# Two of a pair's score groups become one, in an attention and MoE kernel whose order is planned by slots

## The chip, the cores and the metric

The kernel runs on one core of a Trainium2 chip. The metric is the device time of one execution in microseconds; shorter is better.

## The reference

For 4 batches and 8 heads, with 576 tokens and 64 values a head, the kernel computes causal softmax attention and a read of a memory, mixes them by a gate of each head, and sends the result through two products with a gelu between them.

```python
scores = where(causal, -1e9, q @ k.T / sqrt(64))
a = exp(scores - scores.max(-1)); a /= a.sum(-1) + 1e-9
local = a @ v
q_p = where(q > 0, q, exp(q) - 1) + 1
mem_out = (q_p @ M_prev) / (q_p @ z_prev + 1e-6)
x = g * mem_out + (1 - g) * local        # g = sigmoid(beta), one for each head
h = x @ w_in                             # 2304 x 512 by 512 x 2048
out = (h * sigmoid(1.702 * h)) @ w_out   # 2048 to 512
```

All inputs and the output are float32; the two weights reach the kernel as 64-bit words, from which it decodes float32 itself.

## The kernel before

Attention is worked in 16 pairs of heads (4 batches, 4 pairs in each). The two heads of a pair lie on the two halves of the partitions, so that the scores of head 0 and of head 1 use the upper and the lower 64 rows of TensorE and can run beside each other. A pair's queries are cut in blocks of 128: block `i` (0 to 3) sees `128 * (i + 1)` keys, and the last 64 queries of both heads form a tail of 288 + 288 keys. For the first batch blocks 0 and 1 are done by a separate start, so its four pairs (0 to 3, called `rest` in the code) have only blocks 3 and 2 and the tail.

For each block there are scores into a bank of PSUM for each head (`s_both`, tile `ps`), a masked maximum on DVE (`max_unit`, line 560, tile `nm`), an exponential with its sum on ACT (`exp_unit`, line 566, tile `a`), the reciprocal of the sum on DVE (`inv_unit`, tile `sm`), and a scaling on POOL (`scale_unit`, line 569). Then the blocks are transposed on TensorE in units named 0 to 3, "b", "c" and "d" (`tr_unit`, line 139, tile `pt`), each unit in a bank, and copied to SBUF (`ev_unit`, tiles `e`, `eb`, `ec`, `ed`) by DVE ("V") or ACT ("A"). Last come the values (`pv_both`, tile `po`): those for queries 256 on with `js` 0 to 3, then those for queries 0 to 255 with `js` -1. `xboth` takes them from PSUM into a high part `xh` (ACT) and a low part `xl` (DVE).

The first MoE product (tile `pm`, called fill) runs between: eight chunks of 256 or 320 tokens, 16 blocks of w_in (tile `wi`) each, 12 matmuls a block, copied out as `hk` and stored. A chunk can start when the four pairs of its batch have their values. After attention the rest of the fill runs, then the second product (tile `acc`, line 1019).

Order is planned by slots. A pair `p` starts at slot `k0`; pairs 0 to 3 are 7 slots apart, later ones 8. `at(slot, priority, fn)` puts work in a slot. After the events of a slot, fill is handed out until the planner's estimate of TensorE's time for that slot is reached (`PACE`: 2.2 us before slot 60, 2.8 after). Each group of scores counts 0.3 us in that estimate beside its matmuls, and a transpose 0.109. The order in which each engine gets its instructions is then made by a scheduler that simulates the engines; a group has a raised priority, and its matmuls are chained in order. For the chunk of number 1, fill may not run more than four slots ahead.

`scores` (line 719) makes a group: it takes the banks (`s_rooms`), waits with its first matmul for the evictions of the banks before (`rooms(KEEP)`, all but the last one), and takes the values handed on by `hand_on` (line 728) for the pair before behind its own matmuls. Those values wait for all the copies `ev` that they read. `flush` makes a group of values that no scores have taken. The score and transpose banks are four (`ps_s`), and from slot 35 on a fifth (`ps_x`).

Of the kernel before, what the change touches and what calls it, by code (L numbers as in the profile page):

```python
# [34 lines left out]
def tile_attention_memory_moe(ctx, tc, kq, vq, mem, zz, beta, w_in, w_out, out):  # L35
# [46 lines left out]
    def bank(name):  # L82
        state["bank"] += 1
        own = state["slot"] > CONV[-1] + 8 and state["bank"] % 5 == 4
        t = (ps_x if own else ps_s).tile([128, 512], F32, name=name, tag="ps")
        banks.append(id(t))
        held[id(t)] = t
        return t
# [7 lines left out]
    def rooms(keep):  # L96
        return [users[k] for k in banks[:len(banks) - keep][-6:] if k in users]
# [5 lines left out]
    def group(fns, behind):  # L103
        state["group"] = []
        with tc.high_priority(offset=400):
            for fn in fns:
                fn()
        seq = state.pop("group")
        for name in behind:
            if name is not None:  # L110
                tc.add_manual_dep(seq[0].ins, name, SYNC, reason="group")
        for a, b in zip(seq, seq[1:]):
            tc.add_manual_dep(b.ins, a.ins.name, NOSYNC, reason="group")
        state["pe"] += 0.3

    def at(slot, prio, fn):
        assert slot > state["slot"], (slot, state["slot"])
        state["seq"] += 1
        events.setdefault(slot, []).append((prio, state["seq"], fn))
# [451 lines left out]
    def plan_attend(p):  # L571
        b, c = pairs[p]
        k0 = K0[p]
        P = prep[p]
        U = {}
        rest = b < MB
        qo = 256 if rest else 0

        def s_rooms(blocks):
            names = rooms(KEEP)  # L580
            ps = [bank("ps") for _ in range(2)]
            for h in range(2):
                for i in blocks:
                    o = 256 if i == 0 else 0
                    U["ps", h, i] = ps[h][:, o:o + 128 * (i + 1)]
                    U["in", h, i] = ps[h]
            return names

        def s_both(i):
            n, q0 = 128 * (i + 1), S + 128 * i - qo  # L590
            kq = raws[p]["kq"]
            for h in range(2):
                r = slice(64 * h, 64 * h + 64)
                mm(U["ps", h, i], kq[r, q0:q0 + 128], kq[r, :n], True, True)

        def max_unit(h, i):
            n = 128 * (i + 1)
            U["nm", h, i] = softmax_max([(U["ps", h, i][:, :n], n, mask[:, 512 - n:])])

        def exp_unit(h, i):  # L600
            n = 128 * (i + 1)
            if h == 0:
                state["sum"] = (state["sum"] + 1) % 8
                U["sm", i] = sums[state["sum"]]
            if i == 3:
                a = wkp.tile([128, 512], F32, name="a3", bufs=4)
            elif i:
                t = U["t", h, i] = wkp.tile([128, 384], F32, name="a2", bufs=5)
                a = t[:, :n]
            else:  # L610
                a = U["t", h, 1][:, 256:]
            U["a", h, i] = a
            x = softmax_exp(U["ps", h, i][:, :n], a, U["nm", h, i], U["sm", i][:, h, :1])
            used(U.get(("in", h, i), U["ps", h, i]), x)
            state["exp"] = state["late A"] = x.ins.name

        def inv_unit(i):
            sm = U["rs", i] = sml.tile([128, 2], F32, name="sm")
            nc.vector.tensor_reduce(out=sm, in_=U["sm", i], op=ALU.add, axis=AX.X)
            nc.vector.reciprocal(out=sm, in_=sm)  # L620

        def scale_unit(h, i):
            hh = 2 * c + h
            scale_rows(U["a", h, i], U["rs", i][:, h:h + 1], g1[:, hh:hh + 1])
# [42 lines left out]
        def ev_unit(u, eng):  # L667
            n, pt = 128 * len(blocks_of(u)), U["pt", u]
            e = U["e", u] = att.tile([128, n], F32, name=f"e{u}")
            x = copy(eng, e, pt[:, :n])  # L670
            used(pt, x)
            U["ev", u] = state["late " + eng] = x.ins.name
# [32 lines left out]
        def xboth(ch):  # L705
            n = 2 * b + ch
            if n not in xq:
                new_x(n)
            values["po"] = split_sum(n, c, U["po", ch][:, :chunks[n][2]]).ins.name
            if c == NP - 1:  # L710
                xplan[n] = state["slot"] + 1
# [7 lines left out]
        def scores(blocks):  # L719
            names = s_rooms(blocks)  # L720
            late = values.pop("next", None)
            fns = [lambda i=i: s_both(i) for i in blocks]
            if late is not None:
                fns += late[0]
                names = names + late[1]
            group(fns, names)

        def hand_on(js, pv, names):
            values["next"] = ([lambda j=j: pv(j) for j in js], names + [values.get("po")])
# [3 lines left out]
            if late is not None:  # L733
                group(*late)

        for i, idx in ((3, 1), (2, 5)) if rest else ((3, 1), (2, 4), (1, 5), (0, 5)):
            if i:
                at(k0 + idx, 20, lambda i=i: scores((1, 0) if i == 1 else (i,)))
            k = k0 + idx
            for h in range(2):  # L740
                at(k + 1, 10, lambda h=h, i=i: max_unit(h, i))
                at(k + 1, 25, lambda h=h, i=i: exp_unit(h, i))
            at(k + 1, 90, lambda i=i: inv_unit(i))
            for h in range(2):
                at(k + 2 + (h if i >= 2 else 0), 10, lambda h=h, i=i: scale_unit(h, i))
        units = [(0, 8, "V"), (1, 8, "A"), (2, 9, "V"), (3, 9, "A"), ("b", 10, "V"), ("c", 11, "A")]
        if not rest:
            units.append(("d", 12, "V"))
        for u, k, eng in units:
            at(k0 + k, 20, lambda u=u: tr_unit(u))  # L750
            at(k0 + k, 24, lambda u=u, eng=eng: ev_unit(u, eng))
        for js, us, k in ((range(4), (0, 1, 2, 3, "b", "c"), 12), ((-1,), ("c", "d"), 13))[:1 if rest else 2]:
            at(k0 + k, 12, lambda js=js, us=us: hand_on(js, pv_both, [U["ev", u] for u in us]))
            at(k0 + k, 30, flush)
            at(k0 + k, 32, lambda ch=int(js != (-1,)): xboth(ch))
# [84 lines left out]
    for p in range(NPAIRS):  # L840
        plan_prep(p)
        plan_attend(p)
# [113 lines left out]
    units = [(gr, s, p) for gr in range(NG) for s in range(7) for p in range(4)]  # L956
# [82 lines left out]
    k = 0  # L1039
    while fill["gen"] is not None or conv_q or events:  # L1040
# [4 lines left out]
        if k in soon:  # L1045
            t, p = soon[k]
# [120 lines left out]
```

## Time and profile before

| | us |
|---|---|
| median of 3 runs | 608.57 |
| lowest, highest | 608.16, 611.19 |
| the profiled execution | 608.29 |
| its span, first to last instruction | 606.4 |

| engine | busy us | share of the span |
|---|---|---|
| PE (TensorE matmul) | 579.6 | 96% |
| PEld (its weight loads) | 522.4 | 86% |
| DVE | 417.8 | 69% |
| ACT | 348.3 | 57% |
| POOL | 215.9 | 36% |

Times in rows are microseconds from the start of the span. Matmuls are pipelined, so the busy time of a row of them is longer than the step from its start to the start of the next row; the step is what a piece of work takes from the queue. The granted clock of TensorE is 1.00 of full speed in every stretch from 36 us on. Attention runs to about 366 us, the rest of the fill to about 425, the second product to the end.

### The profile page before, as it was taken

What the parts mean: (1) busy time and instruction counts of PE and PEld (TensorE: products, weight loads), DVE (VectorE), ACT (ScalarE), POOL (GpSimd) and SP (SyncE); (2) the same over time, 40 slices, a digit from 0 to 9 for tenths busy, and PEclk for the clock granted to TensorE, in tenths of its full rate; (3) what the DMA queues carried; (4) which work ended last, traced back from release to release, by engine and by line L of the source; (5) the groups of instructions that cost most, each with busy time, mean ns of one, the idle gap of its engine ahead of it and who ended that gap; (6) DMA issues with size and microseconds to landing.
All of it is one profiled execution on the core that took longest, in us unless ns stands there. A gap on an engine that the chain in (4) does not pass through costs nothing.

```text
span 606.4 us, 12121 instructions
## 1 busy us (share of the span) xinstructions
PE 579.6 (96%) x4416; PEld 522.4 (86%) x4416; DVE 417.8 (69%) x998; ACT 348.3 (57%) x791; POOL 215.9 (36%) x279
## 2 busy tenths in 40 slices
PE   4798989999999999999999999999999999999997
PEld 3467777878787888888888899999899999999997
DVE  5878885665669666677555426589698679666964
ACT  6787885655456545545544414466675865676441
POOL 4866664445326433345333213031402301320000
PEclk9599999999999999999999999999999999999999
DMA  8985331344245535455212146521644823471002
GB/s 260 348 302 192 120 120 55 112 138 127 55 165 198 160 100 182 109 202 185 93 65 66 45 144 213 177 98 66 202 132 134 275 83 108 152 222 42 26 1 78
DMA packets 46987, 84.15 MB, mean 139 GB/s; under 512 B 5328, under 2 KB 33232, under 8 KB 46928
## 3 DMA queue, kind: packets, MB, share of 16 engines
q1 hardware_dynamic: 40688, 61.36, 30.7%
q0 software_dynamic: 6240, 22.02, 12.0%
q8 instruction: 34, 0.56, 0.4%
q14 instruction: 25, 0.20, 0.1%
HBM read 59.77 MB, written 23.59 MB: 137 GB/s over the span
## 4 chain that ended last, share of the span: by engine, by line
PE 83%; DVE 5%; ACT 5%; POOL 4%; issue 2%; DMA 1%; SPq 0%; POOLq 0%; DVEq 0%; ACTq 0%
PE pm L130 31%; PE acc L1019 28%; PE ps L130 9%; PE po L130 8%; PE pt L139 6%; ACT a L566 1%; DVE ps L560 1%; POOL a L569 1%; ACT ws L219 1%; POOL wi L152 1%; DMA wraw<-in_w_in_dram 1%; POOL qmt L152 1%; DMA gb<-in_beta_dram 0%; PE pm L424 0%; PE po L424 0%
## 5 line engine op out<-in xcount | busy, mean ns | idle before, releaser
L130 PE MATMUL pm<-xh,wi 128*128 128x320 f32 (+1 forms) x1024 | 219.2, 304 | 3.2 <-POOL wi L152 2.4
L130 PEld LDWEIGHTS pm<-xh,wi 128*128 128x128 f32 x1024 | 164.4, 189 | 9.8 <-POOL wi L152 3.8
L1019 PE MATMUL acc<-oh,wo 128*128 128x384 f32 x672 | 167.9, 336 | 0.5 <-ACT oh L144 0.5
L130 PE MATMUL pm<-xl,wi 128*128 128x256 f32 (+1 forms) x512 | 151.2, 296 | 0.6 <-DVE xl L152 0.6
L1019 PEld LDWEIGHTS acc<-oh,wo 128*128 128x128 f32 x672 | 121.3, 188 | 0.9 <-ACT oh L144 0.9
L569 POOL TENSOR_SCALAR a<-a,sm,g 128x512 f32<-128x512 f32 (+3 forms) x112 | 77.3, 701 | 120.5 <-DVE sm L620 78.0
L1019 PE MATMUL acc<-ol,wo 128*128 128x384 f32 x336 | 109.8, 338 | 0.7 <-DVE ol L152 0.7
L152 DVE TENSOR_TENSOR ol<-g,oh 128x768 fp32r<-128x768 f32 x84 | 79.7, 956 | 37.0 <-ACT oh L144 36.7
L130 PEld LDWEIGHTS pm<-xl,wi 128*128 128x128 f32 x512 | 96.4, 189 | 1.0 <-DVE xl L152 0.8
L566 ACT ACTIVATE a<-ps,nm 128x256 f32<-128x256 f32 (+2 forms) x112 | 59.7, 539 | 63.6 <-DVE nm L560 63.4
L560 DVE CUSTOM_DVE_ANT_0 ps<-ps,mask 128x256 f32<-128x256 f32 (+4 forms) x144 | 67.8, 505 | 41.0 <-PE ps L130 40.2
L144 ACT ACTIVATE oh<-g 128x768 fp32r<-128x768 f32 x84 | 69.9, 841 | 42.1 <-PE acc L1019 32.2
L962 POOL DMA_DIRECT2D g<-gd x48 | 34.8, 726 | 110.5 <-DVE ol L152 61.3
L130 PE MATMUL ps<-kqf 128*128 128x288 f32 (+4 forms) x288 | 67.8, 476 | 5.4 <-ACT ec L144 3.7
L1019 PEld LDWEIGHTS acc<-ol,wo 128*128 128x128 f32 x336 | 62.8, 188 | 1.8 <-DVE ol L152 1.8
L144 ACT ACTIVATE hk<-pm 128x256 f32<-128x256 f32 (+1 forms) x76 | 30.7, 408 | 43.2 <-PE pm L130 39.1
L968 ACT ACTIVATE g<-g 128x768 f32<-128x768 f32 x48 | 39.7, 839 | 16.1 <-DMA g<-gd 12.7
L139 PE MATMUL pt<-ident,a 128*128 128x128 f32 x296 | 48.2, 275 | 0.0
L152 DVE TENSOR_TENSOR g<-g,g 128x768 f32<-128x768 f32 x48 | 45.5, 953 | 1.8 <-ACT g L968 1.8
L130 PEld LDWEIGHTS ps<-kqf 64*128 64x128 f32 (+1 forms) x288 | 30.1, 189 | 17.2 <-ACT ec L144 5.7
L139 PEld LDWEIGHTS pt<-ident,a 128*128 128x128 f32 x296 | 35.0, 140 | 10.6 <-issue 6.8
L147 DVE COPY hk<-pm 128x320 f32<-128x320 f32 (+1 forms) x52 | 23.7, 457 | 23.2 <-PE pm L130 19.0
(138 smaller groups left out, 796.6 us busy)
## 6 DMA issues: line engine op xcount, KB each, us to landing
g<-gd POOLq DMA_DIRECT2D x48, 384.0 KB, 4.5
gd<-hk SPq DMA_DIRECT2D x64, 160.0 KB, 2.5
wraw<-in_w_in_dram SPq DMA_DIRECT2D x16, 512.0 KB, 6.7
gd<-hk SPq DMA_DIRECT2D x64, 128.0 KB, 1.8
kqf<-in_kq_dram SPq DMA_DIRECT2D x12, 608.0 KB, 5.7
vr<-in_vq_dram SPq DMA_DIRECT2D x16, 320.0 KB, 4.9
wraw<-in_w_out_dram SPq DMA_DIRECT2D x10, 512.0 KB, 4.2
qr<-in_vq_dram SPq DMA_DIRECT2D x12, 320.0 KB, 3.1
```

Of the source, the lines that this page charges most:

```text
L130: x = nc.tensor.matmul(out, l, r, start=start, stop=stop)
L139: state["att"] = nc.tensor.transpose(out, in_, idn).ins.name
L144: return nc.scalar.activation(out=dst, in_=src, func=AF.Copy, **kw)
L147: return nc.vector.tensor_copy(dst, src)
L152: return (nc.vector if eng == "V" else nc.gpsimd).tensor_tensor(out=dst, in0=a, in1=b, op=op)
L219: x = nc.scalar.activation(out=box["s"], in_=box["raw"][:, :, 1].bitcast(F32), func=AF.Copy, scale=2.0 ** -112)
L560: nc.vector.tensor_tensor_reduce(out=ps, in0=ps, in1=mk, op0=ALU.add, op1=ALU.min, scale=-0.125, scalar=1e38 if j == 0 else nm[:, j - 1:j] ...
L566: return nc.scalar.activation(out=a, in_=ps, func=AF.Exp, scale=-1.0, bias=nm, accum_out=sm)
L569: return (nc.vector if eng == "V" else nc.gpsimd).tensor_scalar(out=a, in0=a, scalar1=r, scalar2=gcol, op0=ALU.mult, op1=ALU.mult)
L962: x = nc.gpsimd.dma_start(t, gd[4 * kh + p][:, :, t0:t0 + QN].rearrange("i p t -> p i t"))
L968: x = nc.scalar.activation(out=t, in_=t, func=AF.Gelu_apprx_sigmoid)
L1019: nc.tensor.matmul(acc[b, j][:, :QN], W[2 * p + kk][:, WPART[i], sp, 128 * j:128 * j + 128], mv[:, kk], start=first and p + kk == 0 and sp ...
```

## The change

In each pair the scores of blocks 3 and 2 form one group, with four banks, at slot `k0 + 3` (`k0 + 4` in pairs 0 to 3). Before, block 3 had a group at `k0 + 1`, and block 2 one at `k0 + 4` (`k0 + 5` in pairs 0 to 3). Maxima, exponentials, reciprocals and scalings follow the scores with the same distance in slots. Transposes and copy of unit "c" go from slot `k0 + 11` to `k0 + 10`, and the values of keys 0 to 3 are handed on at `k0 + 11` in place of `k0 + 12`, which is the slot of the next pair's new group. Blocks 1 and 0, the tail, the other units and the values for `js` -1 keep their slots. `s_rooms` takes the banks block by block.

```diff
         def s_rooms(blocks):
             names = rooms(KEEP)
-            ps = [bank("ps") for _ in range(2)]
-            for h in range(2):
-                for i in blocks:
-                    o = 256 if i == 0 else 0
-                    U["ps", h, i] = ps[h][:, o:o + 128 * (i + 1)]
-                    U["in", h, i] = ps[h]
+            for i in blocks:
+                for h in range(2):
+                    t = U["in", h, i] = bank("ps") if i else U["in", h, 1]
+                    o = 0 if i else 256
+                    U["ps", h, i] = t[:, o:o + 128 * (i + 1)]
             return names
...
-        for i, idx in ((3, 1), (2, 5)) if rest else ((3, 1), (2, 4), (1, 5), (0, 5)):
-            if i:
-                at(k0 + idx, 20, lambda i=i: scores((1, 0) if i == 1 else (i,)))
+        for i, idx in ((3, 4), (2, 4)) if rest else ((3, 3), (2, 3), (1, 5), (0, 5)):
+            if i in (1, 3):
+                at(k0 + idx, 20, lambda i=i: scores((i, i - 1)))
...
-        units = [(0, 8, "V"), (1, 8, "A"), (2, 9, "V"), (3, 9, "A"), ("b", 10, "V"), ("c", 11, "A")]
+        units = [(0, 8, "V"), (1, 8, "A"), (2, 9, "V"), (3, 9, "A"), ("b", 10, "V"), ("c", 10, "A")]
...
-        for js, us, k in ((range(4), (0, 1, 2, 3, "b", "c"), 12), ((-1,), ("c", "d"), 13))[:1 if rest else 2]:
+        for js, us, k in ((range(4), (0, 1, 2, 3, "b", "c"), 11), ((-1,), ("c", "d"), 13))[:1 if rest else 2]:
```

## Rows read from the trace of the kernel before

**Rows 1.** Busy time by stretch: stretch, us, then each engine's busy us (instructions).

```profile
36.00:92.00 56.00, 50.13 (x439) 40.88 (x440) 47.55 (x125) 45.39 (x115) 37.11 (x38) 1.00 0.53 179
92.00:366.00 274.00, 269.99 (x2412) 233.02 (x2411) 166.30 (x545) 136.20 (x395) 111.14 (x138) 1.00 0.39 122
```

**Rows 2.** The chain that ended last, shares of the span by engine.

```profile
PE 83%; DVE 5%; ACT 5%; POOL 4%; issue 2%; DMA 1%; SPq 0%; POOLq 0%; DVEq 0%; ACTq 0%
```

**Rows 3.** Timeline of PE around block 3's scores, pair 12: start, duration, instruction, count.

```profile
284.77 0.40 PE L130 MATMUL pm<-xh,wi 128*128 128x256 f32 x2
285.00 0.28 PE L130 MATMUL pm<-xl,wi 128*128 128x256 f32 x1
285.21 1.13 PE L130 MATMUL ps<-kqf 64*128 64x512 f32 x4
...
286.27 0.66 PE L139 MATMUL pt<-ident,a 128*128 128x128 f32 x4
```

**Rows 4.** Timeline of PE, pair 12: the other groups of scores.

```profile
291.28 0.92 PE L130 MATMUL ps<-kqf 64*128 64x384 f32 x4
292.13 0.76 PE L130 MATMUL po<-qpt,ms 128*64 128x320 f32 x4
...
294.93 0.76 PE L139 MATMUL pt<-ident,qp 128*128 128x128 f32 x5
...
298.45 0.92 PE L130 MATMUL ps<-kqf 64*128 64x256 f32 x8
```

**Rows 5.** Waits of PE, 92 to 366 us: total us, times, longest.

```profile
PE ps L130 <- ACT ec L144: 2.7, 2, 1.4
```

**Rows 6.** Timeline of PE, pair 5, before block 2's scores: idle time in brackets.

```profile
133.45 1.53 PE L139 MATMUL pt<-ident,a 128*128 128x128 f32 x12
136.33 0.92 PE L130 MATMUL ps<-kqf 64*128 64x384 f32 x4 [1.35 <-ACT ec L144]
```

**Rows 7.** Timeline of ACT, pair 5.

```profile
134.35 0.69 ACT L566 ACTIVATE a<-ps,nm 128x512 f32<-128x512 f32 x1 [1.84 <-DVE nm L560]
...
135.69 0.59 ACT L144 ACTIVATE ec<-pt 128x512 f32<-128x512 f32 x1
...
140.09 0.44 ACT L144 ACTIVATE xh<-po 128x320 fp32r<-128x320 f32 x1 [0.92 <-PE po L130]
```

**Rows 8.** Timeline of PE, block 3's scores of pair 4.

```profile
94.13 1.12 PE L130 MATMUL ps<-kqf 64*128 64x512 f32 x2
...
96.67 1.12 PE L130 MATMUL ps<-kqf 64*128 64x512 f32 x2
```

**Rows 9.** Instructions by line and shape, 92 to 366 us: count | busy us, mean ns | idle before.

```profile
L569 POOL TENSOR_SCALAR a<-a,sm,g 128x512 f32<-128x512 f32 x24 | 20.4, 860 | 52.9 <-DVE sm L620 24.3 <-ACT ec L144 18.7 <-ACT r L869 9.9
...
L566 ACT ACTIVATE a<-ps,nm 128x512 f32<-128x512 f32 x24 | 16.4, 685 | 24.3 <-DVE nm L560 24.2
...
L560 DVE CUSTOM_DVE_ANT_0 ps<-ps,mask 128x512 f32<-128x512 f32 x24 | 16.2, 712 | 24.3 <-PE ps L130 24.3
...
L566 ACT ACTIVATE a<-ps,nm 128x384 f32<-128x384 f32 x24 | 13.8, 577 | 27.6 <-DVE nm L560 27.6
...
L560 DVE CUSTOM_DVE_ANT_0 ps<-ps,mask 128x384 f32<-128x384 f32 x24 | 13.0, 580 | 7.4 <-PE ps L130 7.3
```

**Rows 10.** Timeline of DVE, pair 5: the low part of the values.

```profile
140.57 0.49 DVE L152 TENSOR_TENSOR xl<-po,xh 128x320 fp32r<-128x320 f32 x1 [1.00 <-ACT xh L144]
```

**Rows 11.** Waits of PE, 36 to 92 us.

```profile
PE pm L130 <- POOL wi L152: 2.4, 3, 1.0
PE ps L130 <- ACT ec L144: 1.0, 2, 0.6
```

**Rows 12.** Instructions by line and shape on PE, 366.2 to 426 us.

```profile
L130 PE MATMUL pm<-xh,wi 128*128 128x320 f32 x160 | 35.4, 310 | 0.0
L130 PE MATMUL pm<-xl,wi 128*128 128x320 f32 x80 | 24.7, 309 | 0.0
```

**Rows 13.** Timeline of PE, after pair 7's last values.

```profile
187.75 0.51 PE L130 MATMUL pm<-xl,wi 128*128 128x256 f32 x2 [0.57 <-DVE xl L152]
```

## The prediction

> **What bounds the kernel now.** I read the busy time by stretch first [rows 1]: from 92 to 366 us, where attention for pairs 4 to 15 and the first MoE product share the engines, TensorE (PE) is busy 269.99 of 274 us, while DVE has 166.30, ACT 136.20 and POOL 111.14. From 36 to 92 us (pairs 0 to 3, and the decoding of w_in) nothing is free: PE 50.13 of 56, DVE 47.55, ACT 45.39. Then the chain that ended last [rows 2]: PE holds 83% of it. So after 92 us a microsecond taken out of PE's queue comes off the end, as long as PE has something else to do at once; before 92 us it does so only in part.
>
> What PE's time buys is seen in its timeline. Block 3's scores stand alone between MoE matmuls and transposes [rows 3]. Two MoE matmuls start 0.23 apart, 0.12 each, so after the one at 285.00 the next could have started at 285.12; the scores start at 285.21 and the next transpose at 286.27. The group takes 1.15 us of the queue. Block 2's scores, 384 columns, take 0.85 from their start to the first value matmul [rows 4]: 291.28 to 292.13. The 128 columns between 384 and 512 cost 1.06 - 0.85 = 0.21, so 512 columns are worth 4 x 0.21 = 0.85 and the rest is fixed: 0.21 inside and 0.09 at the entry, 0.30 together. Blocks 1 and 0 go in one group, 256 and 128 columns, and show the same 0.92 of busy time as 384 columns in one block (298.45 beside 291.28): a second block in a group pays no fixed part again. That is the lever of the change.
>
> **The change, part by part.** Blocks 3 and 2 of a pair become one group; the group that block 3 had for itself is gone. All matmuls stay: 4 x 512 and 4 x 384 columns, 52 value matmuls. Per pair one fixed part is saved, 0.30. Pairs 4 to 15 lie in the stretch that PE bounds: 12 x 0.30 = 3.6 us. Pairs 0 to 3 lie where several engines bind; bounds 0 and 4 x 0.30 = 1.2, and I take the middle, 0.6, as PE is busy nine tenths there.
>
> The eviction of "c" moves a slot sooner with its transposes, and so do the values of keys 0 to 3 of the pair before; between transposes and group there is one slot, as before. But block 3 no longer stands in that slot. Today ACT runs block 3's two exponentials, from 134.35, and only then copies "c" at 135.69 [rows 7]; PE finished its transposes before 135 and sat idle 1.35 us until the scores at 136.33 [rows 6]. This happened twice, 2.7 us in all [rows 5]. In the new order no exponentials of block 3 stand ahead of "c". The copy itself, 0.59, and its handover stay, and with block 3 gone PE has 1.06 less to do in that gap. So the gain lies between 0 and 2.7; I take half, 1.4.
>
> Once, at 94.13 and 96.67, the two heads' scores of block 3 stand apart with MoE matmuls between them [rows 8], and each takes 1.12, as long as both take together at 285.21 (1.13). If the new group is not split so, 1.1 us more is gained; if it is split in other places, as much is lost. I count nothing and keep 1.1 either way for the range.
>
> Now what is added. The group needs four score banks at its first matmul instead of two. Banks rotate over five from pair 5 on (over four before), and the fifth is that of "c", whose eviction the values need anyhow; the banks of the transposes before it were evicted earlier. So no new wait at the entry, as long as those evictions keep their place. Behind the group it is different: four maxima, 2 x 0.71 and 2 x 0.58 = 2.58 on DVE, and four exponentials, 2 x 0.69 and 2 x 0.58 = 2.54 on ACT [rows 9], now come in one burst. With the group's start at T, block 3's scores are there at T + 1.06, block 2's at T + 1.70 and the values end at T + 4.50, as the values take 2.80, from 292.13 to 294.93 [rows 4]. The first exponential starts about T + 1.9 (1.06, a maximum of 0.71, a handover) and the last ends about T + 4.5: the values hide the burst almost exactly. Then come nine transposes ("d" and the queries), 0.11 each in the planner (the trace has twelve in 1.53, the last one's tail with them, [rows 6]), to T + 5.5. The next group, blocks 1 and 0, waits for block 2's banks (T + 4.5), for the copy of "d", and for the values to leave PSUM: 0.48 for xh on ACT until xl starts, 0.49 for xl [rows 7, 10], again T + 5.5. So the cover is used up to the last tenth. Queued behind that waiting group on PE are the pair's values for key -1 and MoE matmuls; the scheduler can put MoE matmuls ahead of the group where some are in hand, and cannot where it has run out of them. Bounds: 0, and 0.44 (one ACT copy ahead of xh, [rows 7]) in each of 12 pairs, 5.3. I take 1.0: waits of that size in two or three pairs where MoE matmuls are short, since from 92 to 366 us PE today waits only 4 us in all [rows 1].
>
> No DMA moves. The next pair's loads keep their slots. POOL's scalings of block 3 come two slots later and those of block 2 one sooner (three later and one sooner in pairs 0 to 3); 0.86 each for block 3 [rows 9]. After 92 us POOL is busy 111 of 274 us, so this is hidden; before 92 us see the second rival.
>
> The sum, on the profiled execution's 608.29 us (span 606.4 and 1.89 around it; the three timed runs have a median of 608.57, 0.3 above): 608.29 - 3.6 - 0.6 - 1.4 + 1.0 = 603.7 us.
>
> **Rivals.** First, the saving is handed on to another wait in the same stretch. The planner charges 0.3 us for a group, so with 12 groups fewer after slot 34 it hands out 3.6 us more of MoE matmuls ahead of 366 us. At the end that does no harm: after 366 us 240 matmuls of width 320 are left [rows 12], 192 of the last chunk and 48 of the one before it, 48 x 0.15 = 7.2 us in hand (0.12 for width 256 [rows 3], in proportion). But up to 188 us, where chunk 2 waits for the last values of pair 7, PE already runs short (0.57 us for xl at 187.75, [rows 13]), and there the saving of pairs 4 to 7 (1.2) and of the "c" wait (1.4) can be lost, and the early 0.6 too: 608.29 - 2.4 + 1.0 = 606.9. The short queue speaks for it; that later chunks start without a gap speaks against it for pairs 8 to 15.
>
> Second, and on the other side: pairs 0 to 3. Four maxima, four exponentials and then four scalings come in one piece in the stretch where DVE and ACT are busy 85% and 81%, and where PE already waits 2.4 us for decoded weights from POOL and 1.0 for "c" [rows 11]. Those weights go through ACT, DVE and POOL in program order. If the burst (2.5 us) puts off one decoded block per pair by 2.0 us and PE has no other matmul, that is 4 x 2.0 = 8.0: 608.29 - 3.6 + 8.0 = 612.7. It makes the kernel slower by over 0.5% from 1.7 us a pair on. Against it: a pair has seven slots here, 15.4 us at the planner's pace of 2.2, and the path from the group over exponentials (T + 4.5), four scalings (at most 4 x 0.86 = 3.4) and transposes is over at about T + 12.
>
> Third, the banks: the burst is not hidden, and the group of blocks 1 and 0 waits 0.44 in every pair: 608.29 - 3.6 - 0.6 - 1.4 + 5.3 = 608.0. For it speaks that the cover comes out even; against it, that ACT is busy only half the time after 92 us and that MoE matmuls can go ahead. The Trainium skill, "TensorEngine Tiling (Array Packing)", sections PSUM Bottleneck and Gotcha 1: PSUM Pressure, says that row tiling uses more banks and does not speed up their evacuation, so that the copies out of PSUM may become the limit; by that rule this rival is the forecast and the time 608.0, not 603.7. In the stretch as it is now the trace does not bear it out, with ACT at 136.20 and DVE at 166.30 of 274 us.
>
> That the merged group is split by the scheduler, and so does not do what it says, ends beside the first rival, at about 607.
>
> **How the numbers follow.** The forecast has 0.58, the first rival with the split group 0.20, the third 0.12, the second 0.10. The forecast's own range: all gains at their bounds (3.6 + 1.2 + 2.7 + 1.1, no new wait) give 599.7, the small ones (3.6 alone, with 1.0 of waits) 605.7. For 8 in 10 the range goes from 600.0 to 608.6: it takes in both the first and the third rival's times and leaves out the second, a tenth, and the edges of the others. About 0.5%, 3.0 us, is what a measurement of this kernel can tell from no change. Faster by more than that means under 605.5: 0.58 and a little of the first rival, 0.60. Within it: the rest of the first and the third, 0.29. Slower: the second and a mishap in the third, 0.11.
>
> **What would show it.** In the timeline of PE the 512-column scores are followed at once by the 384-column ones, 1.7 us for both instead of 1.15 + 0.85 apart. The chain of waits shows less than 2.7 us of PE on "ec" after 92 us. A new wait of PE at the 256-column scores for ACT "a", "xh" or DVE "xl" is the third rival's sign; longer waits for "wi", and 92 us reached later, the second's; more idle time of PE from 180 to 190 us the first's. The prediction is wrong if the merged scores take over 1.9 us, or if PE's idle time grows by more than 2 us.

## The result, and the profile after

The change makes the kernel slower: 613.74 us, median of 12 runs (611.00 to 617.27), against 609.02 of the kernel before beside it (608.16 to 611.51). The ratio is 1.0072, 95% interval 1.0045 to 1.0098: 0.7%, against a forecast of 603.7 and a range that ended at 608.6. The profiled execution of after took 616.05 us, 2.3 above the median; over the twelve runs the mean granted clock goes from 0.974 to 0.990, with a median of 0.983.

| | before | after |
|---|---|---|
| span of the profiled execution, us | 606.4 | 614.3 |
| PE busy, us | 579.6 | 579.2 |
| PE not busy (span less busy), us | 26.8 | 35.1 |
| granted clock, mean of the span | 0.988 | 0.978 |
| last value matmul of attention starts, us | 366.0 | 372.7 |
| first matmul of the second product starts, us | 424.5 | 429.4 |

The page of after: span, busy time, granted clock in 40 slices, the chain by engine, and the scores' row (busy, mean ns | idle time before them).

```profile
span 614.3 us, 12162 instructions
...
PE 579.2 (94%) x4416; PEld 528.8 (86%) x4416; DVE 415.1 (68%) x999; ACT 349.1 (57%) x790; POOL 212.8 (35%) x279
...
PEclk9699998999989989999999999999899999999999
...
PE 72%; DVE 9%; ACT 6%; issue 5%; POOL 4%; DMA 3%; POOLq 0%; ACTq 0%; DVEq 0%
...
L130 PE MATMUL ps<-kqf 128*128 128x288 f32 (+4 forms) x288 | 60.3, 467 | 4.6 <-DVE eb L147 2.7
```

The scores' row of the page of before:

```profile
L130 PE MATMUL ps<-kqf 128*128 128x288 f32 (+4 forms) x288 | 67.8, 476 | 5.4 <-ACT ec L144 3.7
```

All scores together are busy 60.3 us; they took 67.8 before. So the lever is there. PE's total falls by only 0.4 us. The granted clock is 0.978 for 0.988, and by an estimate from these two figures that makes 579 us of work some 6 us longer. Beside that stand 8.3 us of new idle time: 2.8 between 36 and 100 us, 5.3 between 160 and 240, 2.6 between 430 and 440, and 2.4 less elsewhere. In the chain PE's share goes from 83% [rows 2] to 72%, and DMA's from 1% to 3%.

The timeline of PE in after, one merged group:

```profile
251.59 0.31 PE L130 MATMUL pm<-xl,wi 128*128 128x320 f32 x1
251.83 1.77 PE L130 MATMUL ps<-kqf 64*128 64x512 f32 x8
253.53 0.76 PE L130 MATMUL po<-qpt,ms 128*64 128x320 f32 x4
```

From 251.83 to 253.53 are 1.70 us, where [rows 3] and [rows 4] took 1.06 and 0.85 and an entry more. Of the fifteen groups after 36 us fourteen show 1.77 and none is split.

The waits of PE in after, 92 to 445 us (total us, times, longest):

```profile
PE pt L139 <- ACT at L566: 3.0, 2, 2.7
PE ps L130 <- DVE eb L147: 2.7, 1, 2.7
PE acc L1018 <- ACT hk L144: 2.5, 1, 2.5
PE pt L139 <- DVE e L147: 1.7, 1, 1.7
PE ps L130 <- ACT ec L144: 1.4, 2, 0.7
```

The "ec" waits are half of [rows 5], as forecast. The four above them do not stand in that stretch of the kernel before, and each comes once or twice. The stretches of after that hold them (us, busy us of PE, PEld, DVE, ACT, POOL with instructions, granted clock, DMA share, GB/s):

```profile
60.00:92.00 32.00, 26.63 (x245) 21.28 (x243) 24.26 (x59) 23.53 (x59) 18.96 (x20) 1.00 0.34 102
92.00:100.00 8.00, 5.87 (x33) 5.41 (x34) 3.80 (x11) 3.85 (x10) 4.02 (x4) 0.79 0.36 101
160.00:180.00 20.00, 17.26 (x121) 14.23 (x122) 12.19 (x40) 9.33 (x27) 6.69 (x9) 0.94 0.49 157
...
430.00:435.00 5.00, 2.52 (x11) 2.23 (x10) 5.00 (x9) 2.44 (x3) 0.00 (x0) 0.84 0.29 100
435.00:440.00 5.00, 4.47 (x19) 3.83 (x18) 3.84 (x7) 3.66 (x5) 4.32 (x6) 0.82 0.56 166
```

**Around 168 to 180 us.** The timelines of SP, ACT, DVE and PE in after:

```profile
167.88 0.80 SPq L864 DMA_DIRECT2D wraw<-in_w_out_dram  x2
...
174.76 0.66 ACT L868 ACTIVATE r<-wraw 128x512 f32<-128x512 f32 x1 [3.97 <-DMA wraw<-in_w_out_dram]
175.32 0.58 ACT L144 ACTIVATE e<-pt 128x512 f32<-128x512 f32 x1
175.80 0.59 ACT L144 ACTIVATE ec<-pt 128x512 f32<-128x512 f32 x1
...
175.45 0.43 DVE L852 TENSOR_SCALAR r<-r 128x512 int32<-128x512 int32 x1 [4.44 <-ACT r L868]
175.79 0.68 DVE L147 COPY eb<-pt 128x512 f32<-128x512 f32 x1
...
173.60 0.28 PE L130 MATMUL pm<-xl,wi 128*128 128x256 f32 x1
176.62 2.60 PE L130 MATMUL ps<-kqf 64*128 64x512 f32 x8 [2.74 <-DVE eb L147]
179.15 1.33 PE L130 MATMUL po<-qpt,ms 128*64 128x320 f32 x4
```

These are the loads and the decoding of w_out. `decode` starts every fourth slot from slot 60 on. It makes each load wait for `state["exp"]`, the last block exponential planned so far, which I call its anchor. Four slots later it plans a scaling `r` on ACT, itself ordered behind the last block exponential planned by then, and three bit operations on DVE. With block 3's exponentials two slots later, every second load finds only those of the pair before. Its anchor passes earlier, and the loads leave in twos: here at once, later 3 to 4 us apart (213.29 and 216.83), where the same two are 6 to 10 apart in the kernel before. The scaling of the other load of the two has lost block 3's exponentials as its anchor in the same way. The first load leaves when it did before (167.88 for 167.59), but ACT now reaches its `r` while it is still under way, 6.86 us in the chain of waits; in the kernel before this `r` starts at 176.46, without waiting. The copies "e", "ec" and, through DVE, "eb" stand behind it, and PE waits for "eb". The Trainium skill, "Perfetto Trace Analysis", section Tensor Engine Instruction, states that ACT and DVE are strict FIFO, that is, each works its queue in order; the rows agree, the copies start right behind `r`. The next merged group, at a lower granted clock, takes 2.60 in place of 1.77.

In the kernel before, each of these loads leaves by itself, and `r` stands behind block 3's exponentials (timelines of SP and ACT, before):

```profile
167.59 0.33 SPq L865 DMA_DIRECT2D wraw<-in_w_out_dram  x1
...
176.11 0.33 SPq L865 DMA_DIRECT2D wraw<-in_w_out_dram  x1
...
217.91 0.68 ACT L566 ACTIVATE a<-ps,nm 128x512 f32<-128x512 f32 x1
...
218.57 0.66 ACT L869 ACTIVATE r<-wraw 128x512 f32<-128x512 f32 x1
```

**Around 213 to 222 us** the same happens to the tail's exponentials, in the chain of waits of after (start, us, what):

```profile
213.29 6.84 DMA wraw<-in_w_out_dram
...
220.72 0.58 ACT at L566 x2
...
221.44 1.60 PE pt L139 x8
```

**At the start of the second product**, behind its first four matmuls, PE waits 2.48 us at 432.77. The timeline of PE, and the chain's shares by line from 424 to 440 us, in after:

```profile
429.42 0.86 PE L1018 MATMUL acc<-oh,wo 128*128 128x384 f32 x4
432.77 1.11 PE L1018 MATMUL acc<-oh,wo 128*128 128x384 f32 x4 [2.48 <-ACT hk L144]
```

```profile
by line: DVE wo L152 45.3%; DVE st L152 25.2%; DVE ol L152 10.9%; ACT wo L144 6.7%; DVE hk L147 5.9%; issue 4.5%; PE acc L1018 2.8%
```

The parts of w_out (`wo`, `st`) are made on DVE once attention has ended, while the rest of the fill runs. From the last value matmul to the second product there are 56.7 us of fill in after and 58.5 before, one w_in block (12 matmuls, 1.8 us) less. The copies of fill ("hk") whose banks the second product needs stand on DVE between those parts, and they now come too late.

### The profile page after: what moved, and what is told of

It is laid out like the page before. It is cut to its first block, busy times and chain, and to the rows that moved or that the text cites. A ratio compares the mean times of both kernels' runs of the same rounds, so it can differ in the third digit from the quotient of the medians.

```text
span 614.3 us, 12162 instructions
## 1 busy us (share of the span) xinstructions
PE 579.2 (94%) x4416; PEld 528.8 (86%) x4416; DVE 415.1 (68%) x999; ACT 349.1 (57%) x790; POOL 212.8 (35%) x279
## 4 chain that ended last, share of the span: by engine, by line
PE 72%; DVE 9%; ACT 6%; issue 5%; POOL 4%; DMA 3%; POOLq 0%; ACTq 0%; DVEq 0%
PE acc L1018 28%; PE pm L130 23%; PE po L130 8%; PE ps L130 7%; PE pt L139 6%; DMA wraw<-in_w_out_dram 2%; POOL wi L152 1%; ACT a L566 1%; DVE st L152 1%; DVE wo L152 1%; DVE ps L560 1%; POOL qmt L152 1%; POOL a L569 1%; ACT fa L566 1%; DVE qp L514 1%
## 5 line engine op out<-in xcount | busy, mean ns | idle before, releaser
L130 PE MATMUL pm<-xh,wi 128*128 128x320 f32 (+1 forms) x1024 | 216.5, 304 | 5.6 <-POOL wi L152 2.9
L130 PE MATMUL pm<-xl,wi 128*128 128x320 f32 (+1 forms) x512 | 151.2, 297 | 0.0
L569 POOL TENSOR_SCALAR a<-a,sm,g 128x512 f32<-128x512 f32 (+3 forms) x112 | 73.4, 669 | 106.5 <-ACT a L566 84.4
L130 PE MATMUL ps<-kqf 128*128 128x288 f32 (+4 forms) x288 | 60.3, 467 | 4.6 <-DVE eb L147 2.7
L139 PE MATMUL pt<-ident,a 128*128 128x128 f32 x296 | 49.9, 282 | 2.7 <-ACT at L566 2.7
L130 PEld LDWEIGHTS ps<-kqf 64*128 64x128 f32 (+1 forms) x288 | 30.9, 189 | 20.3 <-issue 10.2
L139 PEld LDWEIGHTS pt<-ident,a 128*128 128x128 f32 x296 | 36.5, 144 | 5.0 <-issue 2.9
```

The costliest lines, as they stand in the source:

```text
L130: x = nc.tensor.matmul(out, l, r, start=start, stop=stop)
L139: state["att"] = nc.tensor.transpose(out, in_, idn).ins.name
L569: return (nc.vector if eng == "V" else nc.gpsimd).tensor_scalar(out=a, in0=a, scalar1=r, scalar2=gcol, op0=ALU.mult, op1=ALU.mult)
```

## The experiments

There are three suspects: the **charge** of 0.3 us that the planner puts on a group and that the merge saves, so that more fill is handed out early; the **anchor** of the w_out loads; **pairs 0 to 3**. Medians in us, ratios to the kernel before beside them; span, clock and PE's columns are of the profiled execution; "fill" is the time from the start of the last value matmul to that of the first one of the second product. e1 and e2 rest on four runs, e3 and e13 on six, the others on 9 to 12. A profiled execution is one of them and can lie off the median: those of e10 and e13 are 3.2 and 2.8 us under it, that of e8 3.1 above.

| kernel | median | ratio (95%) | span | clock | PE busy | not busy | fill |
|---|---|---|---|---|---|---|---|
| after | 613.74 | 1.0072 (1.0045 to 1.0098) | 614.3 | 0.978 | 579.2 | 35.1 | 56.7 |
| e1 after, decode a slot later | 612.85 | 1.0072 (1.0044 to 1.0100) | 610.3 | 0.986 | 575.9 | 34.4 | 56.8 |
| e3 after, four pairs as before | 612.66 | 1.0067 (1.0032 to 1.0103) | 610.2 | 0.982 | 578.0 | 32.2 | 56.8 |
| e12 after, tail as anchor | 612.10 | 1.0041 (1.0023 to 1.0060) | 609.2 | 0.983 | 577.4 | 31.8 | 56.8 |
| e4 after, charge 0.6 | 609.21 | 1.0009 (0.9989 to 1.0029) | 606.3 | 0.989 | 573.2 | 33.1 | 58.5 |
| e15 after, charge 0.9 | 609.90 | 1.0022 (0.9989 to 1.0055) | 606.6 | 0.989 | 573.6 | 33.0 | 60.3 |
| e6 e4 and e1 | 611.37 | 1.0039 (1.0017 to 1.0060) | 610.6 | 0.983 | 579.5 | 31.1 | 58.6 |
| e7 e4, e1 and e3 | 608.55 | 0.9998 (0.9985 to 1.0012) | 608.7 | 0.983 | 580.4 | 28.3 | 58.5 |
| e10 e4 and e3 | 607.80 | 0.9980 (0.9959 to 1.0002) | 602.8 | 0.992 | 575.6 | 27.2 | 58.5 |
| e8 e4, e3 and e12 | 606.32 | 0.9952 (0.9928 to 0.9976) | 607.7 | 0.983 | 579.3 | 28.4 | 58.5 |
| e13 e8, charge 0.9 | 605.18 | 0.9926 (0.9899 to 0.9952) | 600.6 | 0.989 | 574.8 | 25.8 | 60.3 |
| e16 e8, charge 1.2 | 609.30 | 1.0010 (0.9988 to 1.0031) | 609.2 | 0.989 | 577.0 | 32.2 | 63.9 |
| e2 before, block 3 no anchor | 614.20 | 1.0098 (1.0069 to 1.0128) | 609.6 | 0.992 | 581.7 | 27.9 | 58.5 |
| e9 before, one charge less | 609.73 | 1.0024 (1.0009 to 1.0038) | 607.5 | 0.986 | 579.9 | 27.6 | 56.8 |
| e11 before, tail as anchor | 608.47 | 0.9984 (0.9966 to 1.0003) | 606.0 | 0.992 | 579.2 | 26.8 | 58.5 |
| e14 before, charge 0.6 | 609.61 | 1.0014 (0.9991 to 1.0038) | 607.3 | 0.989 | 581.2 | 26.1 | 60.3 |

**e1: the decoding a slot later**, in the kernel after.

```diff
-        at(60 + 4 * i, 58, lambda i=i: decode(i))
+        at(61 + 4 * i, 58, lambda i=i: decode(i))
```

> The changed kernel with the decoding of w_out (loads, scalings, bit operations) one slot later, so that its anchor, the last block's exponential planned so far, is again that of blocks 3 and 2 of the same pair at every second load. Theory A, the anchor: the change moved block 3's exponentials behind the slot in which every second load is planned, so two loads leave together and a scaling sits in ACT's queue ahead of copies and exponentials while its load is under way; both long waits of TensorE (2.7 us near 176 and near 221) and the lower clock behind them go, and the time is 606 to 609. Theory B, the burst of maxima and exponentials, or the first four pairs: nothing moves, 612 to 615. Theory C, the second product starts late because fill was handed out earlier: 612 to 614.

There is no gain; the time forecast by Theory A is missed, although the waits at 176 and 221 us are gone, and with them all waiting of ACT for these loads. Another wait has come: the tail's scores wait for "ed", which stands behind the bit operations. The timelines of PE and DVE in e1:

```profile
181.60 1.61 PE L130 MATMUL ps<-kqf 128*128 128x288 f32 x10 [2.89 <-DVE ed L147]
...
178.84 1.03 DVE L853 SCALAR_TENSOR_TENSOR r<-wraw,r 128x512 int32<-128x512 int32 x1
179.90 1.04 DVE L855 SCALAR_TENSOR_TENSOR r<-wraw,r 128x512 int32<-128x512 int32 x1
180.87 0.68 DVE L147 COPY ed<-pt 128x512 f32<-128x512 f32 x1
```

**e2: the kernel before, with only the anchor moved.**

```diff
-            state["exp"] = state["late A"] = x.ins.name
+            state["late A"] = x.ins.name
+            if i != 3:
+                state["exp"] = x.ins.name
```

> The kernel before with one edit: block 3's exponentials are no anchor for the decoding of w_out any more. All score groups stay as before. Theory A: two long waits of TensorE for copies or exponentials behind a scaling on ACT, and 612 to 616. Theories B and C: within 1 us of the kernel before, 608 to 610.

The anchor alone costs the kernel before 1.0%, without any merge. What it does to ACT is shown too, in ACT's waits for these loads from 160 to 290 us (total us, times, longest) in the kernel before, in after and in e2; e1 has none:

```profile
ACT hk L144 <- DMA wraw<-in_w_out_dram: 1.2, 1, 1.2
ACT r L868 <- DMA wraw<-in_w_out_dram: 15.4, 5, 4.6
ACT r L871 <- DMA wraw<-in_w_out_dram: 11.8, 5, 2.7
```

But the two long waits of PE that Theory A expected are not there: between 160 and 300 us no wait of PE in e2 is over 0.7 us. So the loss of e2 is not explained by them, and its profile accounts for only part of it: 1.1 us more of PE not busy and 2.1 more of busy.

**e3: pairs 0 to 3 as before**, in the kernel after.

```diff
-        for i, idx in ((3, 4), (2, 4)) if rest else ((3, 3), (2, 3), (1, 5), (0, 5)):
-            if i in (1, 3):
-                at(k0 + idx, 20, lambda i=i: scores((i, i - 1)))
+        for i, idx in ((3, 1), (2, 5)) if rest else ((3, 3), (2, 3), (1, 5), (0, 5)):
+            if rest or i in (1, 3):
+                at(k0 + idx, 20, lambda i=i: scores((i,) if rest else (i, i - 1)))
```

"c" and the values go back to `k0 + 11` and `k0 + 12` for pairs 0 to 2.

> The changed kernel with pairs 0 to 3 grouped as before (block 3 and block 2 apart, unit c and the values a slot later for pairs 0 to 2). Theory A: the waits near 176 and 221 stay, 611 to 614, at most 2 us of TensorE's idle time before 100 us won back. Theory B for the first four pairs: 608 to 610. Theory C: 612 to 614.

By itself this changes nothing that can be measured, though PE's idle time falls by 2.9 us. In the chain towards the second product another wait has grown, 1.7 us for "oh" beside the 2.5 for "hk".

**e4: the charge kept**, in the kernel after: where the planner used to charge two groups 0.6 us, the merged one now has 0.6.

```diff
             group(fns, names)
+            if blocks[0] == 3:
+                state["pe"] += 0.3
```

> The changed kernel, but a merged group counts 0.6 us in the planner instead of 0.3, so that no more fill is handed out during attention than before. Theory A: the two waits stay, 612 to 615. Theory C: more fill is left behind attention and covers the preparation of the second product's weights, so the gap at its start is smaller and the time 610 to 612.

This one line takes away nearly the whole loss, 1.0072 to 1.0009. The time is under both theories' ranges. The block of fill is back behind attention (58.5), and the granted clock, under 1.00 in four stretches of after shown above, is 1.00 in all from 36 us on. ACT waits for the loads as long as in after, 15.3 us in five waits, but PE's waits behind them shrink from 2.74 and 2.73 to 1.89 (for "hk", at 174.02) and 1.2 us. PE is still idle 33.1 us.

**e6, e7: combined with a later decoding.** e6 is e4 and e1, e7 is e4, e1 and e3.

> The changed kernel with both single edits: a merged group counts 0.6 us, and the decoding of w_out is planned a slot later. Theory A with C (the anchor's waits and the fill handed out earlier both cost): better than either edit alone, 606 to 609; TensorE's waits of 2.7 us near 176 and 221 gone, a wait of up to 2.9 for the copy of ed left where fill has run short, the gap before the second product as in the kernel before. If the two edits repair the same loss, 609 to 611.

> As the run with charge and decoding, and pairs 0 to 3 grouped as before. If the burst in pairs 0 to 3 costs (theory B for that stretch), 2 to 3 us of TensorE's idle time between 36 and 100 us go, and the time is 604 to 607, under the kernel before. If not, the same time as without this edit.

Both are slower than forecast. The wait for "ed" stays in both at 2.9 us, so the later decoding is no repair. The first four pairs are worth 0.4% here (1.0039 to 0.9998).

One thing stands beside the edits as named: in e7, e8, e10, e13 and e16 the line with the charge also takes the separate group of block 3 in pairs 0 to 3, which is so charged 0.3 us more than in the kernel before (0.6 in e13, 0.9 in e16). What that does was not separated; from 36 to 92 us PE is busy 50.0 us in e10 and 50.2 in e13, as in the kernel before (50.13).

**e9: the kernel before, charged as after.** Block 3's group is charged nothing (the line of e4 with `-= 0.3`).

> The kernel before, with block 3's group counted 0 in the planner in place of 0.3 us, so that it hands out as much fill during attention as the changed kernel does. Theory C: about 3 us more between the end of the fill and the steady second product, 610 to 613. If handing out fill earlier costs nothing: 608 to 609.5.

The time lies between the two ranges. The saved charge costs the kernel before 0.24% and gives it after's wait of 2.5 us for "hk". So handing out fill earlier does harm by itself, but less than in the merged kernel (3.8 us, e4).

**e8: the tail's exponentials anchor too**, with the edits of e4 and e3, decoding at slot 60.

```diff
                 used(U["ps"][f], x)
+            state["exp"] = x.ins.name
```

> As the run with all three, but the decoding stays in its slots and the tail's exponentials become anchors as well. Theory A: the scalings stand behind the tail's exponentials and each load leaves at its own time, so no wait of over 1.5 us for a scaling; and as bit operations no longer stand ahead of the copy of ed, the 2.9 us wait near 181 is gone too: 603 to 607. If it is only the slot that counts and not the anchor, 607 to 610, with the waits near 176 and 221 still there.

It is faster than both kernels and in the range of Theory A, but not by its mechanism: the loads still leave in twos, the first two within 1.6 us, and ACT waits 4.40 us for the first. Only the wait for "ed" stays away. Three more runs take e8 apart.

**e10: e8 without the anchor. e11: the anchor in the kernel before. e12: the anchor alone in the kernel after.**

> The merged kernel with the charge of 0.3 us kept for the merged group and pairs 0 to 3 grouped as before; the decoding of w_out keeps its slots and its anchor. Theory (the charge is worth about 4 us, the first four pairs about 1, the anchor the rest): about 608.0, ratio to the kernel before 0.996 to 1.002, with idle time of PE of about 3 us in 160 to 200 us and over 1 us in 200 to 240 us. Rival (the anchor costs nothing once the charge is kept): as fast as the version that also lets the tail's exponentials anchor the loads, ratio 0.993 to 0.997.

> The kernel before, in which the tail's exponential also counts as the last one planned for the loads of w_out. Theory (in the kernel before every load already follows block 3's exponentials a slot earlier, so the anchor is not late there): no change, ratio 0.998 to 1.002, and the gain of the merged version with the tail's anchor is the merge's own. Rival (the later anchor is worth 2 to 3 us by itself): ratio 0.994 to 0.997.

> The kernel after, in which the tail's exponential also counts as the last one planned for the loads of w_out; the charge and pairs 0 to 3 stay as in the kernel after. Theory (charge first): the waits behind the scaling near 176 and 221 us shrink, those before the second product stay over 2 us, 611 to 613, ratio 1.003 to 1.007. Rival (the anchor alone is the cause): 607 to 609, ratio under 1.000.

e11 shows that the edit is worth nothing that can be measured without the merge. In e12 the kernel after has 0.3% less with it, and e8 has 0.3% less than e10; the intervals overlap in both, so a gain by this anchor is not shown. e10 shows that the charge and the four pairs alone already reach the time of before.

**e13, e14, e15, e16: more charge.** 0.9 us for the merged group in e8, 0.6 for block 3's in before, 0.9 in after, 1.2 in e8.

> The merged version with the tail's anchor and pairs 0 to 3 as before, in which the merged group is charged 0.9 us where two groups were charged 0.6 before. Theory (what counts is that as much fill is left behind attention as in the kernel before; more than that is worth nothing): within 0.3% of the version with 0.6, ratio 0.993 to 1.000, with the first matmul of the second product near 424 us. Rival (any fill held back is worth as much again): another 3 to 4 us, ratio 0.988 to 0.991. Other rival (the pace now ends too early in fill and attention ends later): ratio over 1.000.

> The kernel before, in which block 3's group is charged 0.6 us instead of 0.3. Theory (fill held back only pays where the merge has opened waits; the kernel before has few): within 0.2%, ratio 0.998 to 1.002, idle time of PE near 11 us as before. Rival (the kernel before was paced too fast, and the charge speeds up any version): 605 to 607, ratio 0.993 to 0.997.

> The kernel after, whose merged group is charged 0.9 us, and nothing else. Theory (the charge covers the waits behind the anchor and before the second product, pairs 0 to 3 keep their loss of 1 to 2 us): 605.5 to 608, ratio 0.995 to 0.999. Rival (without the tail's anchor the waits near 176 us stay whatever the charge): 608.5 or more, ratio 1.000 or more.

> The merged version with the tail's anchor and pairs 0 to 3 as before, the merged group charged 1.2 us. Theory (idle time of PE is down to that of the kernel before with 0.9 already): within 0.3% of the version with 0.9, ratio 0.990 to 0.996. Rival (too little fill between the groups, so waits for copies and exponentials come back): ratio over 0.997.

e13 has the lowest median of the study, 0.7% under before. It lies within 0.3% of e8, as its theory said, just under that theory's range, and the intervals of the two overlap, so that 0.9 is better than 0.6 is not shown. Its page, the waits of PE and the timelines of SP, ACT and PE:

```profile
span 600.6 us, 12158 instructions
...
PE 574.8 (96%) x4416; PEld 524.1 (87%) x4416; DVE 416.3 (69%) x998; ACT 348.0 (58%) x791; POOL 212.6 (35%) x279
```

```profile
PE ps L130 <- ACT ec L144: 1.9, 3, 0.8
...
PE ps L130 <- DVE eb L147: 0.3, 1, 0.3
```

```profile
163.78 1.29 SPq L867 DMA_DIRECT2D wraw<-in_w_out_dram  x2
...
168.15 0.67 ACT L871 ACTIVATE r<-wraw 128x512 f32<-128x512 f32 x1 [2.08 <-DMA wraw<-in_w_out_dram]
...
170.75 1.77 PE L130 MATMUL ps<-kqf 64*128 64x512 f32 x8 [0.29 <-DVE eb L147]
```

Two loads still leave together, but ACT waits 2.08 us and not 3.97, and PE waits 0.29. PE is not busy for 25.8 us in all (26.8 before), and at nearly the same clock its busy time is 4.8 less: with the new waits mostly gone, the time that the merge saves reaches the end. In this execution that makes 5.8 us of the span; by the medians it is 3.5. One wait that goes with the larger charge can be named: with a charge of 0.6 (e4, e6, e7, e8, e10) PE still waits 1.7 us for "hk" at the start of the second product, with 0.9 (e13, e15) it does not.

e14 refutes the rival that more charge speeds up any version: the kernel before stays where it was. In e15 and e16 it is the theory that fails and the rival that holds. e15: without the other two edits 0.9 brings after only to the time of before, and the waits behind the scalings stay ("at" 2.5 us, "eb" 1.0 at the longest). e16: with 1.2 the gain of e13 is lost again, at the same place, in the chain of waits:

```profile
162.49 5.63 DMA wraw<-in_w_out_dram
...
168.14 0.67 ACT r L871
...
170.50 0.68 DVE r L858
171.18 0.41 DVE hk L147
...
171.64 1.33 PE pm L130 x9
```

PE waits 3.53 us there for a bank of fill ("hk"), whose copy stands on DVE behind the decoding.

## Why the prediction was wrong

On the two spans, 7.9 us apart, the sum's -3.6 and -0.6 became -0.4 of PE's busy time, and its -1.4 and +1.0 became +8.3 of idle time. By the prediction's own sign (idle time up by more than 2 us) it was wrong.

**The lever was right, and so was its size.** The merged scores take 1.70 us of the queue where the two groups and the entry took 2.00, the 0.30 of the forecast. Forecast were 3.6 + 0.6 for the fixed cost. In the five merged kernels whose clock was as high as before's 0.988 or higher (e4, e10, e13, e15, e16), PE is busy 573.2 to 577.0 us, which is 2.6 to 6.4 under before's 579.6; the middle one, e13, has 4.8 less (with twelve merged groups, as e10 and e16). The 0.6 for pairs 0 to 3 was not collected: there PE's idle time grew, as said under the second rival.

**The granted clock had no term in the sum.** The prediction does not mention it. In after it falls behind gaps of PE, 0.978 for 0.988 in the profiled executions; in the medians it is 0.983 for 0.989 (before, in the runs beside e1 to e4), by an estimate 0.6% or 3 to 4 us.

**The half of the "ec" waits was right**: 1.4 us saved, 1.4 left, in the same two places (0.69 for 1.35 each). That it was just the middle of the stated bounds is luck; e13 has 1.9 left.

**"No DMA moves" failed.** The loads of w_out and their scalings are ordered behind exponentials, and those moved. I looked at loads that have slots of their own and did not follow what else depends on a block's exponentials. The sum needed a term for it. In the merged kernel PE's waits behind these scalings are 2.74 and 2.73 us, at 176 and 221 us, without what the lower clock adds. That the moved anchor makes ACT wait is shown by e2 (and by e1, which takes it back); that it costs the kernel before 1.0% is measured, but by which way is open. How much of ACT's waiting becomes PE's waiting differs from kernel to kernel: e4 has as much of the first as after and 3.1 us of the second in place of 5.5.

**The term of +1.0 for new waits failed with it**, in its place and its size. It was put behind the group, at blocks 1 and 0, for "xl" or "a". In the list of after no scores wait for "xl", and those for "a" have 0.2 us before 100 us. So the third rival did not happen either. The rule that row tiling raises the pressure on PSUM (the Trainium skill, "TensorEngine Tiling (Array Packing)", Gotcha 1: PSUM Pressure) did not decide here: the group of blocks 1 and 0 never waited for the burst. What failed is "no new wait at the entry, as long as those evictions keep their place": at 176.62 the merged group waits 2.74 us at its entry, for "eb", which DVE copied late. The large waits after 160 us lie where a copy stands on ACT or DVE behind work of another stage.

**The first rival's "at the end that does no harm" failed.** The charge was seen, but I asked only whether PE would have fill left, and 48 spare matmuls said yes. What the fill covers was the question: the making of w_out on DVE, behind the end of attention. One block less uncovers 2.5 us, in e9 as in after. e4 shows that the charge is worth most of the loss, 3.8 us; of that the wait at the second product explains only a part, as 1.7 of its 2.5 us stay. Another part lies between 92 and 240 us, where PE's idle time goes from 10.2 to 8.4 us and the granted clock from 0.96 and 0.97 to 1.00. That the forecast left out this rival's other place, 180 to 190 us, turned out well: PE is idle 0.5 us there in after, 1.3 before.

**The second rival** had the right sign and place, and a price several times too high: PE is idle 2.8 us more from 36 to 100 us (8.69 for 5.87), not 8.0; the wait for "wi" from ACT grew from 0.2 to 2.2 us. Taking that part back gave 0.05% alone (nothing), and 0.3 to 0.4% once the charge was kept (e4 to e10, where the intervals overlap, and e6 to e7, where they do not).

**What stays open.** The edits do not add up: the same charge of 0.9 gives 0.9926 with the other two and 1.0022 without, and 1.2 loses what 0.9 gained. A new charge moves every instruction against the loads and the copies, so it seems that a kernel's time depends on where a few coincidences fall; the single waits of PE seen here are 2 to 4 us. That is argued from the traces, no run shows it by itself. Which part of e13's gain is the charge's and which the luck of these places was not separated. For e2 the profile holds only part of the loss, and no long wait of PE.

## What to carry to other kernels

When a step is moved, search the program for everything that takes it as an anchor: loads, scalings and estimates that are "behind the last one planned" move without appearing in the diff. When work in a planned order becomes cheaper, its charge in the planner should be lowered only if the work that is handed out in its place is not cover for something later; try the old charge first. A gain on the bounding engine is collected only if its idle time stays as it was, so compare busy and not-busy time apart.

## What the runs showed of the hardware

- In after the granted clock fell behind gaps of PE: to 0.79 from 92 to 100 us, after PE had been idle 5.37 of 32 us, and to 0.94, 0.84 and 0.82 in the other stretches shown above (means over the two levels, 1.2 and 2.4 GHz). A gap can so cost more than its own length: behind the wait of 2.74 us the merged group took 2.60 us in place of 1.77. The clock does not always fall: e4 is idle 5.35 of those same 32 us and has 1.00 behind it.
- From two 512 KB loads issued together on SP to the scaling that waited for the first of them 6.86 us passed in after, some 4.4 in e13 (163.78 to 168.15). Leaving together is not all of it: the load of 213.29 in after, 3.5 us ahead of the next, took 6.84. The median of these loads from issue to landing was 4.9 us in after, 4.2 in before.
